# Seven late blocks of a SwiGLU down-projection by Strassen's seven products

## The chip, the core and the metric

The kernel runs on one core of a Trainium2 chip. Its engines work side by side and wait for each other by semaphores: TensorE (PE in the profile; PEld is its loading of weights), VectorE (DVE), ScalarE (ACT), GpSimd (POOL), and SyncE (SP), which here only starts DMAs. Matrix products go from SBUF into PSUM; VectorE and ScalarE read PSUM, GpSimd does not. The metric is device time in microseconds, lower is better. Before the change the median of three runs is 863.33 us (863.15 to 863.42).

## The reference

The input x is 8 batches of 3008 tokens with 256 channels. Each batch goes through a global filter along the tokens, then every token through a gated feed-forward layer:

```python
X = np.fft.rfft(x, axis=1)
Y = X * (filt_r + 1j * filt_i)[None]
y = np.fft.irfft(Y, n=x.shape[1], axis=1)          # (8, 3008, 256)

xn = y / sqrt(mean(y * y, -1) + 1e-6) * rms_g      # per token
g, val = xn @ w_gate, xn @ w_val                   # 256 -> 1536
out = (silu(g) * val) @ w_out                      # 1536 -> 256
```

The result is float32; the kernel's operands for matrix products are fp16 with fp32 sums.

## The kernel before

The filter is a two-stage Fourier transform (47 by 64) by matrix products with constant tables: `a_unit`, `b_unit` with `s_part` and `add_unit` (the multiplication by the filter), `bi_unit`, `n_unit`. It then squares and scales (`sq_unit`, `stat_unit`, `xt_unit`) and transposes by DMA (`tr_unit`) into `xn`, the feed-forward layer's input. This runs one batch ahead of the feed-forward layer and is woven into it.

The feed-forward layer is a list of 576 items (line 718): batch b (8), block m (6 per batch, 512 tokens each as four columns of 128; the last block of an even batch has three), inner tile jt (12 of 128 units, `JT`). One turn of the loop from line 837 handles a slot i:

- `gv(b, m, jt)` (line 533): two products of 512 columns each for gate and value (contraction 256 in two steps) into `pg` and `pv`, one PSUM bank each, two buffers each; Silu on ScalarE into `sg` (line 550); `hh = pv * sg` on VectorE (line 551), 128 inner units by 512 tokens, fp16, four buffers in turn.
- the units that the plan holds for this slot.
- `down` of the item two slots back (line 554): for each of the four token columns one product with `hh`'s 128x128 part as stationary operand and a row of `w_out` (256 columns) as the moving one, summed over jt in two PSUM banks `po0` and `po1`, which have one buffer each. The first one of a block is put off to the next slot, so that the banks' previous sums can be read out. After the twelfth, ScalarE copies one bank (line 568) and VectorE the other (line 569) into `o3`, and `o_store` puts the DMA to the output in SP's queue at a later slot.

The order of the work is fixed when the program is made. The plan (lines 718 to 830) gives each unit a slot, with costs per engine in microseconds in `load` and a limit per slot in `room`; a unit that does not fit moves to a later slot. Each engine takes its instructions in that order.

Memory: the pool `stg` has four buffers of 8 KB per partition. They hold the filter and gate and value weights during the load (`f_load`, `w_load`, both by DMAs from GpSimd's queue), later the fp32 tiles `y`, which use the first half of a buffer only (line 170). From line 610 the start is written out by hand; there `w_load(1)` stands behind `w_load(0)` (line 629).

The costliest names in the profile are line 546 (products of gate and value), 563 (down-projection), 551, 550, and on GpSimd 268 (`add_unit`), 330, 332 (`stat_unit`) and 340 (`xt_unit`).

Of the kernel before, what the change touches and what calls it, by code (L numbers as in the profile page):

```python
# [10 lines left out]
FP32 = mybir.dt.float32  # L11
FP16 = mybir.dt.float16
AXT = mybir.ActivationFunctionType
ALU = mybir.AluOpType
# [6 lines left out]
P = 128  # L21
D = 256
B = 8
DFF = 1536
JT = DFF // P
# [8 lines left out]
XC = 6  # L34
NXC = H // XC
KC = 8


def _make_tables():
# [62 lines left out]
def kernel(  # L102
# [11 lines left out]
    nc = tc.nc  # L114
# [6 lines left out]
    z_d = nc.dram_tensor("z_tmp", (B, K2, KR, D), FP16, kind="Internal").ap()  # L121

    glob = ctx.enter_context(tc.tile_pool(name="glob", bufs=1))
    stg = ctx.enter_context(tc.tile_pool(name="stg", bufs=4))
    xp = ctx.enter_context(tc.tile_pool(name="xp", bufs=4))
    t1p = ctx.enter_context(tc.tile_pool(name="t1p", bufs=3))
    t2p = ctx.enter_context(tc.tile_pool(name="t2p", bufs=3))
# [7 lines left out]
    hp = ctx.enter_context(tc.tile_pool(name="hp", bufs=4))  # L135
    op = ctx.enter_context(tc.tile_pool(name="op", bufs=2))
    psG = ctx.enter_context(tc.tile_pool(name="psG", bufs=2, space=bass.MemoryType.PSUM))
    psV = ctx.enter_context(tc.tile_pool(name="psV", bufs=2, space=bass.MemoryType.PSUM))
    psO = ctx.enter_context(tc.tile_pool(name="psO", bufs=1, space=bass.MemoryType.PSUM))
# [12 lines left out]
    wg = glob.tile([P, 2, DFF], FP16)  # L152
    wv = glob.tile([P, 2, DFF], FP16)
    wo = glob.tile([P, JT, D], FP16)
    gsb = glob.tile([P, 2], FP32)
    hhs = [glob.tile([P, 512], FP16, name="hh%d" % i) for i in range(4)]
    ss3 = [glob.tile([P, 4, 2, P], FP16, name="ss%d" % i) for i in range(3)]
# [6 lines left out]
    st = {b: {"x": {}, "t1": {}, "t2": {}, "s": {}, "yt": {}, "t4": {}, "y": {}, "sq": {},  # L164
              "u": {}, "xn": {}} for b in range(B)}

    def raw(src, row, ap):
        return bass.AP(tensor=src.tensor, offset=src.offset + row * D, ap=ap)

    def y_tile():  # L170
        t = stg.tile([P, 2, 4, 256], FP32, tag="stg", name="y")
        return t.rearrange("p a b c -> p (a b c)")[:, 0:1024].rearrange("p (a e) -> p a e", a=2)

    def x_load(b, c):
        t = xp.tile([P, XC, D], FP16, tag="xc", name="xc")
# [37 lines left out]
    def t2_tile(b, c):  # L213
        if b == 0 and c == 3:
            st[b]["t2"][c] = op.tile([KR, KC, D], FP16, tag="o3", name="t2o")
        else:
            st[b]["t2"][c] = t2p.tile([KR, KC, D], FP16, tag="t2", name="t2")

    def t2_load(b, c):
        t2_tile(b, c)  # L220
        nc.sync.dma_start(st[b]["t2"][c], z_d[b, c * KC:(c + 1) * KC, :, :].rearrange("k p d -> p k d"))

# [13 lines left out]
    def b_unit(b, i, bk=3, e=0):  # L236
        g, dh = divmod(i, 2)
        ps = bank(bk, "psb")[:, 0:4 * KR]
        for k in range(4):
            kk = 4 * g + k  # L240
            nc.tensor.matmul(ps[:, ts(k, KR)], st[b]["t2"][kk // KC][:, kk % KC, ds(dh * P, P)],  # L241
                             wb[0:KR, kk, :], start=True, stop=True)
# [128 lines left out]
        copy(eng, st[0]["t2"][c][:, 4 * r:4 * r + 4, :].rearrange("p k (e d) -> p k e d", e=2), ps)  # L371

    fst = {}
    FR4 = 4

    def f_load(i, f):
        if i not in fst:
            fst[i] = stg.tile([P, 2, FR4, D], FP32, tag="stg", name="fs")
        t = fst[i]
        row = FR4 * P * i if i < 2 else NF - 1 - FR4 * P  # L380
        for src in ((filt_i, filt_r)[f],):
            nc.gpsimd.dma_start(t[:, f].rearrange("p a d -> p (a d)"),
                                raw(src, row, [[FR4 * D, P], [1, FR4 * D]]))

    def f_unit(i, f, dh, e):
        t = fst[i]
        ps = bank(1 + "AV".index(e), "psf").rearrange("p (a q) -> p a q", a=FR4)
        for a in range(FR4):
            nc.tensor.transpose(ps[:, a, :], t[:, f, a, ds(dh * P, P)], idf)  # L389
        v = ps.rearrange("p a (q s) -> p s a q", s=16)  # L390
        fk = ff[:, dh, 0:K2].rearrange("p (t k) c -> p t k c", k=4)
        fu = ff[:, dh, 1:K2 + 1].rearrange("p (t k) c -> p t k c", k=4)[:, ::-1, ::-1, :]
        lo = SL * (1 + f) + 8 * i
        hi = lo + H
        if i < 2:
            copy(e, fk[:, :, :, lo:lo + 8], v[:, 0:8])
            copy(e, fu[:, :, :, hi:hi + 8], v[:, 8:16])
        else:
            copy(e, fk[:, :, :, lo:lo + 8], v[:, 8:16])
            copy(e, fu[:, :, :, hi:hi + 7], v[:, 0:8, :, 1:8])  # L400
# [6 lines left out]
    def f_neg(k0, n, dhs=(0, 1)):  # L407
        for dh in dhs:
            nc.gpsimd.tensor_scalar(out=ff[:, dh, k0:k0 + n, 0:SL], in0=ff[:, dh, k0:k0 + n, SL:2 * SL],
                                    scalar1=-1.0, scalar2=1.0, op0=ALU.mult, op1=ALU.mult)  # L410
# [102 lines left out]
    def scale_apply(m, bk):  # L513
# [12 lines left out]
                                    in1=y[:, h, :].rearrange("p (q e t) -> p q e t", q=2, e=2), op=ALU.mult)  # L526
        st[0]["xn"][m] = xn

    SPLIT = ((0, 0, 0), (B - 1, 5, JT - 1))
    hh_of = {}  # L530
    po_of = {}

    def gv(b, m, jt):
        n = nq(b, m)
        xn = st[b]["xn"][m]
        parts = ((0, 2), (2, 4)) if (b, m, jt) in SPLIT else ((0, n),)
        sg = hp.tile([P, 512], FP16, tag="sg", name="sg")
        hh = hhs[(6 * JT * b + JT * m + jt) % 4]
        made = []
        for q0, q1 in parts:  # L540
            w = (q1 - q0) * P
            pg = psG.tile([P, 512], FP32, tag="pg", name="pg")
            pv = psV.tile([P, 512], FP32, tag="pv", name="pv")
            for ps, wt in ((pg, wg), (pv, wv)):
                for dt_ in range(2):
                    nc.tensor.matmul(ps[:, 0:w], wt[:, dt_, ts(jt, P)], xn[:, q0:q1, dt_, :],  # L546
                                     start=(dt_ == 0), stop=(dt_ == 1))
            made.append((pg, pv, w, slice(q0 * P, q1 * P)))
        for pg, pv, w, c in made:
            nc.scalar.activation(out=sg[:, c], in_=pg[:, 0:w], func=AXT.Silu)  # L550
            nc.vector.tensor_tensor(out=hh[:, c], in0=pv[:, 0:w], in1=sg[:, c], op=ALU.mult)  # L551
        hh_of[(b, m, jt)] = hh

    def down(b, m, jt):
        hh = hh_of.pop((b, m, jt))
        if jt == 0:
            po_of[(b, m)] = [psO.tile([P, 2, D], FP32, tag="po%d" % i, name="po%d" % i)
                             for i in range(2)]
        po = po_of[(b, m)]

        n = nq(b, m)
        for s4 in range(n):
            nc.tensor.matmul(po[s4 // 2][:, s4 % 2, :], hh[:, ts(s4, P)], wo[:, jt, :],  # L563
                             start=(jt == 0 and s4 % 2 == 0),
                             stop=(jt == JT - 1 and (s4 % 2 == 1 or s4 == n - 1)))
        if jt == JT - 1:
            o3 = op.tile([P, 4, D], FP32, tag="o3", name="o3")
            nc.scalar.activation(out=o3[:, 0:2, :], in_=po[0], func=AXT.Copy)
            nc.vector.tensor_copy(out=o3[:, 2:n, :], in_=po[1][:, 0:n - 2, :])
            po_of[(b, m)] = o3  # L570
# [18 lines left out]

    def w_load(q):  # L590
        cols = ts(q, DFF // 3)
        t = stg.tile([P, 2, 2, DFF // 3], FP32, tag="stg", name="ws")
        for src, k in ((moe_w_gate, 0), (moe_w_val, 1)):
            nc.gpsimd.dma_start(t[:, k], src.rearrange("(dt p) j -> p dt j", p=P)[:, :, cols])
        wst[q] = t
# [14 lines left out]
    with tc.manual_schedule():  # L610
# [15 lines left out]
        nc.gpsimd.dma_start(wb[:, 0:4, :], wb_d[:, 0:4, :])  # L626
        nc.gpsimd.dma_start(wi, wi_d)
        w_load(0)
        w_load(1)
        nc.vector.memset(mhalf, -0.5)  # L630
        nc.vector.memset(ones, 1.0)
        for t in ss3[1:]:
# [29 lines left out]
        for g in range(7):  # L662
            tr0_unit(g, "V")
            if g < 6:
                f_unit(*todo[g + 2], "A")
        f_neg(4, 4, (0,))
        f_neg(8, 8, (0,))
        UN = K2 // 2
# [49 lines left out]
        items = [(b, m, jt) for b in range(B) for m in range(6) for jt in range(JT)]  # L718
        plan, late = {}, {}
        front = (sq_unit, s_part, add_unit)  # L720
        load = {r: [0.0] * (len(items) + 99) for r in "MBAV"}
        room = {"A": 0.8, "V": 0.7}
        for i in range(JT + 1, len(items), JT):
            load["A"][i] = 0.6
            load["V"][i] = 0.68

        def at(slot, fn, *a):
            todo = (late if fn == q_unit else plan).setdefault(slot, [])
            if fn in front:
                todo.insert(0, (fn, a))  # L730
            else:
                todo.append((fn, a))
# [77 lines left out]
        for b in range(1, B):  # L810
            t = (b - 1) * 72
# [20 lines left out]
        for i, now in plan.items():  # L832
            if any(fn == a_unit and a[3] == 0 for fn, a in plan.get(i + 1, ())) and bi_unit in [fn for fn, _ in now]:
                now.sort(key=lambda u: u[0] == sq_unit)

        stores = {}
        for i in range(len(items) + 4):
            if i < len(items):
                gv(*items[i])
            for fn, a in plan.pop(i, ()):  # L840
                fn(*a)
            if 2 <= i < len(items) + 2:
                b, m, jt = items[i - 2]
                if jt == 1 and i > JT:
                    down(b, m, 0)
                if jt or i < JT:
                    down(b, m, jt)
                if items[i - 2][2] == JT - 1:
                    stores[i + 1] = items[i - 2][:2]
            for fn, a in late.pop(i, ()):  # L850
                fn(*a)
            if i in stores:
                o_store(*stores[i])
# [31 lines left out]
```

## Time and profile before

| what | value |
|---|---|
| median of three runs | 863.33 us |
| span of the profiled execution (first to last instruction) | 861.4 us |
| PE, PEld busy | 852.4, 532.2 us |
| DVE, ACT, POOL busy | 557.2, 612.4, 297.8 us |
| mean granted TensorE clock | 0.999 |
| DMA | 107.98 MB, mean 125 GB/s |

The page lists no time of the profiled execution beside its span, so the median stands for it: 1.9 us lie around the span. Busy times are sums over the span; engines overlap. In a line of the timeline the columns are start, length in microseconds, engine, line of the kernel, instruction, what it writes and reads with shapes and types, and how many; in square brackets stands the idle time of the engine before it and what ended it. A product's length in these lines includes its way through the array; products that follow one another start sooner than that.

### The profile page before, as it was taken

To read this page: it belongs to the slowest core of one execution; us is meant where nothing else is said; L and a number is where in the kernel's file an instruction comes from. 1 tells how busy PE (TensorE), PEld (TensorE's weight loads), DVE (VectorE), ACT (ScalarE), POOL (GpSimd) and SP (SyncE) were. 2 spreads that over 40 slices of the span, in tenths; PEclk is the share of its full clock that TensorE was granted. 3 is DMA by queue.
4 is the path that set the end of the run, shared out by engine and by line. 5 is a ranking of instruction groups with operands and counts; after the bars stand their busy time and mean duration, and the time that the engine had idled before them with its cause. 6 is when DMAs were issued, how large, how long until landed. Compare 5 with 4: busy or idle time off the path is not lost.

```text
span 861.4 us, 17024 instructions
## 1 busy us (share of the span) xinstructions
PE 852.4 (99%) x6142; PEld 532.2 (62%) x6142; DVE 557.2 (65%) x926; ACT 612.4 (71%) x1339; POOL 297.8 (35%) x346
## 2 busy tenths in 40 slices
PE   8999999999999999999999999999999999999997
PEld 6755666566666666666666666666666666665664
DVE  5857655776666666666666676767666665555554
ACT  4986777787588756887577856888567765777443
POOL 5725742453144322534034430444123430132000
PEclk9999999999999999999999999999999999999999
DMA  9995778765975476656755548433564331521101
GB/s 283 270 204 124 150 164 168 139 130 121 197 137 129 121 150 111 151 107 147 139 127 113 132 98 180 108 87 101 131 127 93 97 70 42 124 54 49 62 25 50
DMA packets 198237, 107.98 MB, mean 125 GB/s; under 512 B 158566, under 2 KB 182520, under 8 KB 198152
## 3 DMA queue, kind: packets, MB, share of 16 engines
q1 hardware_dynamic: 189464, 85.52, 44.1%
q0 software_dynamic: 8544, 21.24, 12.7%
q8 instruction: 48, 0.79, 0.4%
q14 instruction: 37, 0.30, 0.1%
q10 hardware_dynamic: 144, 0.13, 0.0%
HBM read 45.78 MB, written 35.65 MB: 95 GB/s over the span
## 4 chain that ended last, share of the span: by engine, by line
PE 96%; DMA 1%; ACT 1%; DVE 1%; issue 0%; POOL 0%; POOLq 0%
PE po L563 28%; PE pg L546 28%; PE pv L546 28%; PE psb L241 3%; PE psi L285 3%; PE psn L314 2%; PE psa L206 2%; DMA fs<-in_filt_i_dram 1%; PE psy L418 1%; PE psf L389 1%; PE pst L367 0%; ACT sg L550 0%; POOL xc L186 0%; DVE s L231 0%; DVE hh L551 0%
## 5 line engine op out<-in xcount | busy, mean ns | idle before, releaser
L551 DVE TENSOR_TENSOR hh<-pv,sg 128x512 f16<-128x512 f32 (+2 forms) x578 | 391.5, 678 | 286.4 <-ACT sg L550 221.9
L550 ACT ACTIVATE sg<-pg 128x512 f16<-128x512 f32 (+2 forms) x578 | 337.4, 584 | 217.6 <-PE pg L546 213.4
L546 PE MATMUL pg<-xn,wg 128*128 128x512 f16 (+2 forms) x1156 | 338.1, 374 | 0.1
L546 PE MATMUL pv<-xn,wv 128*128 128x512 f16 (+2 forms) x1156 | 338.1, 374 | 0.0
L563 PE MATMUL po<-wo,hh 128*128 128x256 f16 x2256 | 332.7, 273 | 0.0
L563 PEld LDWEIGHTS <-hh 128*128 128x128 f16 x2256 | 213.4, 98 | 105.5 <-issue 0.6
L268 POOL TENSOR_TENSOR ss<-s,s 128x384 f16<-128x384 f16 x112 | 101.9, 911 | 273.2 <-DVE s L234 245.2
L546 PEld LDWEIGHTS <-wv 128*128 128x128 f16 x1156 | 112.9, 98 | 130.7
L546 PEld LDWEIGHTS <-wg 128*128 128x128 f16 x1156 | 111.4, 98 | 17.0 <-issue 0.3
L340 POOL TENSOR_TENSOR xt<-y,rho 128x1024 f16<-128x1024 f32 (+1 forms) x46 | 85.4, 1856 | 2.8
L322 ACT ACTIVATE junk<-y 128x256 f16<-128x256 f32 x180 | 74.3, 413 | 2.8
L231 DVE TENSOR_TENSOR s<-psb,ff 128x384 f16<-128x384 f32 x124 | 67.6, 547 | 0.7 <-ACT ff L195 0.6
L234 DVE TENSOR_TENSOR s<-psb,ff 128x384 f16<-128x384 f32 x124 | 67.6, 546 | 0.0
L195 ACT ACTIVATE uu<-psi 128x384 f16<-128x384 f32 (+1 forms) x127 | 61.6, 486 | 1.5 <-DMA out_dram<-o 0.5
L195 ACT ACTIVATE y<-psn 128x512 f32<-128x512 f32 (+1 forms) x95 | 55.7, 588 | 4.2
L285 PEld LDWEIGHTS <-yt 96*128 96x128 f16 x512 | 35.4, 97 | 26.7 <-issue 1.0
L332 POOL TENSOR_TENSOR rho<-u,mhalf 128x4 f32<-128x4 f32 (+1 forms) x46 | 46.5, 1010 | 3.8
L330 POOL TENSOR_SCALAR u<-ss 128x4 f32<-128x4 f32 (+1 forms) x46 | 8.9, 193 | 104.8 <-ACT junk L322 103.8
L195 ACT ACTIVATE t<-psa 128x512 f16<-128x512 f32 x70 | 41.4, 594 | 3.1 <-PE psa L206 1.7
L285 PE MATMUL psi<-wi,yt 96*128 96x96 f16 x512 | 42.9, 205 | 0.1
L241 PE MATMUL psb<-wb,t 96*128 96x96 f16 x480 | 40.1, 206 | 0.3 <-DVE s L234 0.2
L241 PEld LDWEIGHTS <-t 96*128 96x128 f16 x480 | 28.7, 97 | 12.8 <-DVE s L234 3.3
(101 smaller groups left out, 366.2 us busy)
## 6 DMA issues: line engine op xcount, KB each, us to landing
out_dram<-o SPq DMA_DIRECT2D x40, 512.0 KB, 3.6
xc<-in_x_dram POOLq DMA_DIRECT2D x31, 384.0 KB, 5.6
z_tmp<-t SPq DMA_DIRECT2D x28, 384.0 KB, 2.7
t<-z_tmp SPq DMA_DIRECT2D x28, 384.0 KB, 6.0
out_dram<-o SPq DMA_DIRECT2D x7, 384.0 KB, 2.7
fs<-in_filt_i_dram POOLq DMA_DIRECT2D x3, 512.0 KB, 10.8
fs<-in_filt_r_dram POOLq DMA_DIRECT2D x3, 512.0 KB, 11.2
ws<-in_moe_w_gate_dram POOLq DMA_DIRECT2D x3, 512.0 KB, 9.8
```

What stands on the lines that cost most here:

```text
L195: nc.scalar.activation(out=out, in_=in_, func=AXT.Copy, **({} if scale is None else {"scale": scale}))
L231: eng.tensor_tensor(out=o, in0=ps, in1=f1, op=ALU.mult)
L234: eng.tensor_tensor(out=o, in0=ps[:, :, ::-1, :], in1=f2, op=ALU.mult)
L241: nc.tensor.matmul(ps[:, ts(k, KR)], st[b]["t2"][kk // KC][:, kk % KC, ds(dh * P, P)], wb[0:KR, kk, :], start=True, stop=True)
L268: nc.gpsimd.tensor_tensor(out=ss3[g % 3][:, :, dh, 0:KR], in0=s[0], in1=s[1], op=ALU.add)
L285: nc.tensor.matmul(ps[:, k, :], yt[0:KR, k, dh, :], wi[0:KR, 4 * g + k, :], start=True, stop=True)
L322: nc.scalar.activation(out=junk, in_=y[:, i, ts(u, D)], func=AXT.Square, accum_out=ss[:, 2 * i + u:2 * i + u + 1])
L340: nc.gpsimd.tensor_tensor(out=xt[:, 0:n, :], in0=y.rearrange("p a (u d) -> p (a u) d", u=2)[:, 0:n, :], in1=rho[:, 0:n].unsqueeze(2).to_br ...
L546: nc.tensor.matmul(ps[:, 0:w], wt[:, dt_, ts(jt, P)], xn[:, q0:q1, dt_, :], start=(dt_ == 0), stop=(dt_ == 1))
L550: nc.scalar.activation(out=sg[:, c], in_=pg[:, 0:w], func=AXT.Silu)
L551: nc.vector.tensor_tensor(out=hh[:, c], in0=pv[:, 0:w], in1=sg[:, c], op=ALU.mult)
L563: nc.tensor.matmul(po[s4 // 2][:, s4 % 2, :], hh[:, ts(s4, P)], wo[:, jt, :], start=(jt == 0 and s4 % 2 == 0), stop=(jt == JT - 1 and (s4 ...
```

## The change

In seven blocks, (6,3), (6,4) and (7,0) to (7,4), the items of a block are walked in two halves of two token columns (256 tokens), six pairs of inner tiles each. An item is now two inner tiles by two token columns, and its down-projection, a 2x2 by 2x2 block product (token columns by inner tiles, inner tiles by output halves of 128 channels), is made by Strassen's seven products in place of eight. The number of items, 12 per block, stays.

- `gv_seven` makes the gate and value of an item with eight products of 256 columns, then Silu and hh as before, and three further VectorE instructions, all on fp16 in SBUF: the sums and differences of hh's parts (two of 256 elements per partition, one of 128).
- `w_seven` makes the five sums of parts of `w_out` once, on GpSimd, at slots 372 to 420.
- `down_seven` makes seven products of 128 columns. After a half's last one, ScalarE copies 128 and 512 columns out of PSUM, VectorE makes one sum and GpSimd three to get the output's four parts. The first down-projection of each half is put off by a slot, so the output banks change hands twice a block. The store is issued at slot i+3 where it was i+1.
- The plan's `load` gets 0.56 more on VectorE for each such item and 0.7 on ScalarE once per block.
- The four `stg` buffers become four fixed tiles `big`, used in the same turn; the sums lie in their second halves. `w_load(1)` is issued after the first batch's filter units.

```diff
+    big = [glob.tile([P, 2 * FR4 * D], FP32, name="big%d" % i) for i in range(4)]
+    spare = [t[:, FR4 * D:] for t in big]
+    half = [t.bitcast(FP16) for t in spare]
...
+    SEVEN = {(B - 2, m) for m in (3, 4)} | {(B - 1, m) for m in range(5)}
+
+    def w_seven(n):
+        v = wo.rearrange("p (i j) (e d) -> p i j e d", j=2, e=2)
+        f, a, b = ((ALU.add, (0, 0), (1, 1)), (ALU.subtract, (0, 1), (1, 1)), (ALU.subtract, (1, 0), (0, 0)),
+                   (ALU.add, (0, 0), (0, 1)), (ALU.add, (1, 0), (1, 1)))[n]
+        nc.gpsimd.tensor_tensor(out=ws7[n], in0=v[:, :, a[0], a[1], :], in1=v[:, :, b[0], b[1], :], op=f)
+
+    def gv_seven(b, m, jt):
+        half, jp = divmod(jt, JP)
...
+        for ps, wt in ((pg, wg), (pv, wv)):
+            for j in range(2):
+                for dt_ in range(2):
+                    nc.tensor.matmul(ps[:, ts(j, 2 * P)], wt[:, dt_, ts(2 * jp + j, P)],
+                                     xn[:, 2 * half:2 * half + 2, dt_, :], start=(dt_ == 0), stop=(dt_ == 1))
+        nc.scalar.activation(out=sg, in_=pg, func=AXT.Silu)
+        nc.vector.tensor_tensor(out=hh, in0=pv, in1=sg, op=ALU.mult)
+        a = hh.rearrange("p (s t) -> p s t", s=4)
...
+        nc.vector.tensor_tensor(out=hs[:, 0:2], in0=a[:, 0:2], in1=a[:, 3:4].to_broadcast([P, 2, P]), op=ALU.add)
+        nc.vector.tensor_tensor(out=hs[:, 2:4], in0=a[:, 1:3], in1=a[:, 0:4:3], op=ALU.subtract)
+        nc.vector.tensor_tensor(out=h5, in0=a[:, 0], in1=a[:, 2], op=ALU.add)
+        hh_of[(b, m, jt)] = (a, hs, h5)
+
+    def down_seven(b, m, jt):
...
+        mm(pb[:, 0], a[:, 0], ws7[1][:, jp], **first)
+        mm(pb[:, 1], a[:, 3], ws7[2][:, jp], **mid)
+        mm(pa[:, 0], hs[:, 0], ws7[0][:, jp], **first)
+        mm(pb[:, 3], hs[:, 1], w[:, 0, 0], **mid)
+        mm(pa[:, 2], hs[:, 2], ws7[3][:, jp], **mid)
+        mm(pa[:, 1], hs[:, 3], ws7[4][:, jp], **last)
+        mm(pb[:, 2], h5, w[:, 1, 1], **last)
+        if jp == JP - 1:
+            o = o3_of[(b, m)][:, 2 * half:2 * half + 2, :].rearrange("p q (e d) -> p (q e) d", e=2)
+            t = osum
+            nc.scalar.activation(out=t[:, 4], in_=pa[:, 0], func=AXT.Copy)
+            nc.scalar.activation(out=t[:, 0:4], in_=pb, func=AXT.Copy)
+            nc.vector.tensor_tensor(out=o[:, 0:4:3], in0=pa[:, 1:3], in1=t[:, 4:5].to_broadcast([P, 2, P]), op=ALU.add)
+            nc.gpsimd.tensor_tensor(out=o[:, 1:3], in0=t[:, 0:2], in1=t[:, 2:4], op=ALU.add)
+            nc.gpsimd.tensor_tensor(out=t[:, 2:4], in0=t[:, 1::-1], in1=t[:, 2:4], op=ALU.subtract)
+            nc.gpsimd.tensor_tensor(out=o[:, 0:4:3], in0=o[:, 0:4:3], in1=t[:, 2:4], op=ALU.add)
...
-        w_load(1)
...
+        w_load(1)
         f_neg(4, 4, (0,))
...
+        for b, m in SEVEN:
+            for jt in range(JT):
+                load["V"][6 * JT * b + JT * m + jt] += 0.56
+            load["A"][6 * JT * b + JT * m + JP + 1] += 0.7
...
+        for n in range(5):
+            at(372 + 12 * n, w_seven, n)
...
+                seven = (b, m) in SEVEN
+                fn, n = (down_seven, JP) if seven else (down, JT)
+                if jt % n == 1 and i > JT:
+                    fn(b, m, jt - 1)
+                if jt % n or i < JT:
+                    fn(b, m, jt)
+                if jt == JT - 1:
+                    stores[i + (3 if seven else 1)] = (b, m)
```

More of the change, by code (lines that the diff above doesn't have):

```diff
@@ L36 @@
 KC = 8
+FR4 = 4
 def _make_tables():
@@ L123 @@
     glob = ctx.enter_context(tc.tile_pool(name="glob", bufs=1))
-    stg = ctx.enter_context(tc.tile_pool(name="stg", bufs=4))
     xp = ctx.enter_context(tc.tile_pool(name="xp", bufs=4))
@@ L154 @@
     wo = glob.tile([P, JT, D], FP16)
+    big = [glob.tile([P, 2 * FR4 * D], FP32, name="big%d" % i) for i in range(4)]
+    spare = [t[:, FR4 * D:] for t in big]
+    half = [t.bitcast(FP16) for t in spare]
+    ws7 = [half[n // 2][:, ts(n % 2, JT // 2 * P)].rearrange("p (i d) -> p i d", d=P) for n in range(5)]
+    hs4 = [(half[0][:, 1536:], half[1][:, 1536:], half[3][:, 0:512], half[3][:, 512:1024])[i]
+           .rearrange("p (s t) -> p s t", s=4) for i in range(4)]
+    hs1 = [half[3][:, 1024 + i * P:1024 + (i + 1) * P] for i in range(4)]
+    osum = spare[2][:, 384:1024].rearrange("p (s t) -> p s t", s=5)
     gsb = glob.tile([P, 2], FP32)
@@ L168, in raw, with big_tile @@
         return bass.AP(tensor=src.tensor, offset=src.offset + row * D, ap=ap)
+    turn = [0]
+    def big_tile():
+        turn[0] += 1
+        return big[(turn[0] - 1) % 4]
     def y_tile():
-        t = stg.tile([P, 2, 4, 256], FP32, tag="stg", name="y")
-        return t.rearrange("p a b c -> p (a b c)")[:, 0:1024].rearrange("p (a e) -> p a e", a=2)
+        return big_tile()[:, 0:FR4 * D].rearrange("p (a e) -> p a e", a=2)
     def x_load(b, c):
@@ L373 @@
     fst = {}
-    FR4 = 4
     def f_load(i, f):
         if i not in fst:
-            fst[i] = stg.tile([P, 2, FR4, D], FP32, tag="stg", name="fs")
+            fst[i] = big_tile().rearrange("p (f a d) -> p f a d", f=2, a=FR4)
         t = fst[i]
@@ L527, in scale_apply @@
         st[0]["xn"][m] = xn
+    JP = JT // 2
+    SEVEN = {(B - 2, m) for m in (3, 4)} | {(B - 1, m) for m in range(5)}
[4 more added lines that the diff above has]
+        nc.gpsimd.tensor_tensor(out=ws7[n], in0=v[:, :, a[0], a[1], :], in1=v[:, :, b[0], b[1], :], op=f)
@@ new lines, in gv_seven @@
+    def gv_seven(b, m, jt):
+        half, jp = divmod(jt, JP)
+        xn = st[b]["xn"][m]
+        sg = hp.tile([P, 512], FP16, tag="sg", name="sg")
+        hh = hhs[(6 * JT * b + JT * m + jt) % 4]
+        pg = psG.tile([P, 512], FP32, tag="pg", name="pg")
+        pv = psV.tile([P, 512], FP32, tag="pv", name="pv")
+        for ps, wt in ((pg, wg), (pv, wv)):
[6 more added lines that the diff above has]
+        a = hh.rearrange("p (s t) -> p s t", s=4)
+        n = (6 * JT * b + JT * m + jt) % 4
+        hs, h5 = hs4[n], hs1[n]
+        nc.vector.tensor_tensor(out=hs[:, 0:2], in0=a[:, 0:2], in1=a[:, 3:4].to_broadcast([P, 2, P]), op=ALU.add)
+        nc.vector.tensor_tensor(out=hs[:, 2:4], in0=a[:, 1:3], in1=a[:, 0:4:3], op=ALU.subtract)
+        nc.vector.tensor_tensor(out=h5, in0=a[:, 0], in1=a[:, 2], op=ALU.add)
+        hh_of[(b, m, jt)] = (a, hs, h5)
@@ new lines, in down_seven @@
+    def down_seven(b, m, jt):
+        a, hs, h5 = hh_of.pop((b, m, jt))
+        half, jp = divmod(jt, JP)
+        if jt == 0:
+            o3_of[(b, m)] = op.tile([P, 4, D], FP32, tag="o3", name="o3")
+        if jp == 0:
+            po_of[(b, m)] = [psO.tile([P, 2, D], FP32, tag="po%d" % i, name="po%d" % i)
+                             .rearrange("p a (e d) -> p (a e) d", e=2) for i in range(2)]
+        pa, pb = po_of[(b, m)]
+        first, mid, last = dict(start=(jp == 0), stop=False), dict(start=False, stop=False), \
+            dict(start=False, stop=(jp == JP - 1))
+        w = wo[:, 2 * jp:2 * jp + 2, :].rearrange("p j (e d) -> p j e d", e=2)
+        mm = nc.tensor.matmul
+        mm(pb[:, 0], a[:, 0], ws7[1][:, jp], **first)
[14 more added lines that the diff above has]
+            nc.gpsimd.tensor_tensor(out=o[:, 0:4:3], in0=o[:, 0:4:3], in1=t[:, 2:4], op=ALU.add)
+            po_of[(b, m)] = o3_of[(b, m)]
@@ L529 @@
     SPLIT = ((0, 0, 0), (B - 1, 5, JT - 1))
+    o3_of = {}
     hh_of = {}
@@ L591, in w_load @@
         cols = ts(q, DFF // 3)
-        t = stg.tile([P, 2, 2, DFF // 3], FP32, tag="stg", name="ws")
+        t = big_tile().rearrange("p (k e j) -> p k e j", k=2, e=2)
         for src, k in ((moe_w_gate, 0), (moe_w_val, 1)):
@@ L838 @@
             if i < len(items):
-                gv(*items[i])
+                (gv_seven if items[i][:2] in SEVEN else gv)(*items[i])
             for fn, a in plan.pop(i, ()):
@@ L843 @@
                 b, m, jt = items[i - 2]
[L844 to L849, printed above, removed]
+                seven = (b, m) in SEVEN
[6 more added lines that the diff above has]
+                    stores[i + (3 if seven else 1)] = (b, m)
             for fn, a in late.pop(i, ()):
```

## The prediction

> **What bounds the kernel now.** I read the page first (busy shares, chain of waits), then the busy times of each engine in the stretches that the changed blocks occupy, then single instructions in the timeline for prices.
>
> From the page of the kernel before: span, busy times, chain by engine.
> ```profile
> span 861.4 us, 17024 instructions
> PE 852.4 (99%) x6142; PEld 532.2 (62%) x6142; DVE 557.2 (65%) x926; ACT 612.4 (71%) x1339; POOL 297.8 (35%) x346
> PE 96%; DMA 1%; ACT 1%; DVE 1%; issue 0%; POOL 0%; POOLq 0%
> ```
> TensorE is the bound: it makes 96% of the chain, so a nanosecond off its work counts as long as nobody makes it wait. The reader should also note the other shares: VectorE is idle only a third of the time.
>
> Busy time in five of the seven changed blocks (stretch, its length, then PE, PEld, DVE, ACT, POOL with instruction counts):
> ```profile
> 716.47:732.59 16.12, 16.12 (x109) 9.89 (x108) 9.35 (x15) 9.17 (x16) 1.20 (x2) 1.00 0.20 56
> 732.59:748.73 16.14, 16.14 (x101) 9.71 (x100) 8.92 (x14) 11.13 (x24) 3.10 (x3) 1.00 0.58 125
> 761.43:777.46 16.03, 16.03 (x98) 9.48 (x97) 8.58 (x13) 11.70 (x28) 6.19 (x6) 1.00 0.19 42
> 777.46:793.71 16.25, 16.25 (x100) 9.67 (x99) 8.80 (x13) 11.86 (x28) 3.09 (x3) 1.00 0.26 66
> 809.31:824.91 15.60, 15.60 (x97) 9.38 (x96) 8.90 (x14) 7.76 (x13) 0.00 (x0) 1.00 0.09 34
> ```
> I put the borders at the first Silu of blocks (6,3), (6,4), (7,0), (7,1) and (7,3). (7,2) and (7,4), from 793.71 and 824.91, also last 15.60. TensorE is busy all through at full clock. A bare block is 15.60 us, 1.300 per item; the first four carry 0.43 to 0.65 of other units. VectorE has about 6.7 to 7.5 us free per block: that is the room that the new work has to fit in.
>
> Prices, from the timeline (start, length, engine, line):
> ```profile
> 7.86 1.06 PE L357 MATMUL psa<-tab,xc 128*128 128x128 f16 x16
> 830.34 0.60 PE L563 MATMUL po<-wo,hh 128*128 128x256 f16 x4
> 825.54 0.69 DVE L551 TENSOR_TENSOR hh<-pv,sg 128x512 f16<-128x512 f32 x1 [0.61 <-ACT sg L550]
> 55.31 0.16 DVE L509 CAST hl<-rho 128x4 f16<-128x4 f32 x1
> 55.50 0.16 DVE L510 TENSOR_TENSOR hl<-rho,hl 128x4 f16<-128x4 f32 x1
> 19.99 1.28 DVE L197 COPY t2o<-pst 96x1024 f16<-96x1024 f16 x2 [0.20 <-PE pst L367]
> 26.25 0.55 DVE L234 TENSOR_TENSOR s<-psb,ff 128x384 f16<-128x384 f32 x1
> 26.71 0.55 DVE L231 TENSOR_TENSOR s<-psb,ff 128x384 f16<-128x384 f32 x1
> ```
> Sixteen 128-column products, each with its own weight load, start (1.06 - 0.219)/15 = 0.056 apart. The four 256-column products start (0.60 - 0.273)/3 = 0.109 apart. The 1.300 of an item then leaves (1.300 - 4 x 0.109)/4 = 0.216 for a 512-column product. On VectorE, 384 elements with fp32 operands start 0.46 apart, while 1024 fp16 elements start 1.28 - 0.68 = 0.60 apart: some 0.065 fixed, plus 1.04 ns per element, or half that where all is fp16. Line 510 reads what line 509 wrote and starts 0.03 after its end.
>
> **The change, part by part.** TensorE. An item (two inner tiles by 256 tokens) had four products of 512 columns and four of 256: 1.300. It gets eight of 256 and seven of 128: 8 x 0.109 + 7 x 0.056 = 1.264. That saves 0.036, and over 84 items 3.0 us. Doubling the weight loads of gate and value costs nothing by the 256-column row (one load per product there already); nor do seven loads in the down-projection, by the 128-column row. The Trainium skill speaks against this: "TensorE: Matmul & The Clock Gate", section "Back-to-back issue gap", gives about 81 ns per product for a stream of loads and 128-column products. By that rule the seven would take 0.567, an item 1.439, and the kernel would lose 12 us; this trace, with 56 ns in a stream of just that kind, does not agree, and the measurement decides.
>
> VectorE, per item. Added are two adds of 256 fp16 elements and one of 128, all operands in SBUF. No row has a two-operand fp16 form. One element per step bounds them above: 2 x 0.331 + 0.198 = 0.86. The fixed part alone bounds them below: 3 x 0.065 = 0.20. I take two per step, 2 x 0.198 + 0.132 = 0.53, since the fp16 copy, nearest in type, runs so. The first add reads hh, so it waits for its end: 0.69 + 0.03 instead of 0.61 until VectorE is free. An item is then 0.72 + 0.53 = 1.25. Per block the 512-element copy of the output (0.61) goes and two 256-element adds (0.33 each) come. A block is 12 x 1.25 + 0.66 = 15.66 on VectorE. On TensorE it becomes 0.43 shorter: 15.69, 15.71, 15.60, 15.82 and three times 15.17. So TensorE paces the first four, or nearly; in the three bare blocks VectorE is the longer by 0.49 each. With 0.06 from (7,0) that is 1.5, less what VectorE may lag before anybody waits. That is least at a handover of the output banks, which now comes twice a block: bank po0 is wanted again two gate-value groups and two products later, 2 x 0.872 + 0.11 = 1.86, and in the meantime come the drain (0.17), ScalarE's 128-column copy (some 0.27, from 0.594 for 512 and 0.486 for 384) and, as VectorE gets there about 1.24 after the last product, the 0.33 add: 0.3 spare. 1.5 - 0.3 = 1.2 us come back.
>
> ScalarE. Per half two copies (0.17 and 0.49 to the next start) replace one of 0.49 per block: 0.8 more per block on 7.8 to 11.9 of 16, room enough. But a pair of squares (0.41 + 0.19 each) holds a Silu up to 1 us now, which hh hid in VectorE's idle time. With that idle time gone, part of it comes through: seven pairs in the second run of changed blocks, 0 to 0.3 each, 0 to 2 us; I take 0.9, as hh is then late already and half of it overlaps.
>
> GpSimd. Three fp32 adds of 256 elements per half: xt takes 1.892 for 1024 and 1.465 for 768, so about 0.18 + 256 x 1.67 ns = 0.61 each. They use 4 of 15 us per block beside at most 6.2, feed only the store, and cost nothing by themselves. The five weight sums (768 fp16 elements; 0.911 for 384 makes 1.6 each) fall in slots 372 to 420, ahead of queued ss adds. The yt transposes behind these then land 1.6 later; the one that landed at 596.35 is first read at 600.87, so 4.5 hides 1.6. Without that cover it would be 1.6 each, 8 us.
>
> Queues and places. The store goes two slots later on SP; behind it wait only xn transposes with ten slots to spare. The second weight load keeps its place in GpSimd's queue, after the first load and ahead of line 409's work, and waits for the same readers: nothing. The staging ring has four buffers in the same order; the sums lie in the half that y does not use. Working the planner's formula with the added loads moves no unit. The Silu and hh work itself is unchanged in size.
>
> Sum: -3.0 + 1.2 + 0.9 = -0.9. The span of 861.4 becomes 860.5. The median of the runs shown is 863.33, 1.9 above this span; I leave that as it is: 862.4.
>
> **The rivals.** First, faster: VectorE keeps up everywhere. It decides at (15.17 - 0.66)/12 = 1.21 per item, that is adds 0.04 cheaper than mine together. The fixed part of 0.065 is from instructions with a PSUM operand, and these have none. Then only TensorE's 3.0 counts: 860.4.
>
> Second, slower: GpSimd holds VectorE up. Every VectorE instruction of weight so far has at most one operand in SBUF; each new add has two. If such an add cannot start while a GpSimd instruction runs, then only hh (0.72) covers it. A norm's rho (1.01) and xt (1.89) leave 0.29 + 1.17 = 1.46 or more; five of these sets lie in or at the end of changed blocks: 7.3. The first two output adds (1.22) run beside the 0.33 add and hh (1.05) and leave 0.2, the third, if it gets in between the new adds, 0.6: 0.2 to 0.8 in each of 14 halves, 2.8 to 11. Together 10 to 18, and 873 when the lower end holds. For it: VectorE has no idle time left to take it in. Against it: hh keeps 0.69 beside any GpSimd work, but it has only one SBUF operand, so the trace says nothing for two. The Trainium skill states it: "SBUF — State Buffer", section "SBUF: two separate sides": "The shared pair is an exclusive lock, not a bandwidth split", with a VectorE instruction of two SBUF inputs among those that need it. No row here shows that.
>
> Third, slower: the adds go one element per step. An item is 1.58, a block 19.6, some 4 us more than TensorE's in each of seven: 889. Against it stands the fp16 copy.
>
> Fourth, the output handover misses its 0.3: half a microsecond in 14 halves, 7 us, 869. Against it: line 568 and 569's copies of twice the size held no product up before.
>
> **How the numbers follow.** My forecast (VectorE just at TensorE's pace, 861 to 865) has 0.40; faster 0.22; GpSimd 0.29; one per step 0.05; handover or dearer products 0.04. What a measurement can tell from no change is 0.2%, 1.7 us: 861.6 to 865.1. Of the forecast's 0.40, 0.11 lies below that, 0.23 inside and 0.06 above. So faster 0.33, same 0.23, slower 0.44. The range reaches from the first rival's 860.4 to 876, past the second's 873; above lie the upper half of the second and the third, some 0.15, below 0.04.
>
> **What would show it.** TensorE: products of 256 and 128 columns 0.109 and 0.056 apart, an unheld item of 1.264. VectorE: the 256-element adds near 0.28 long (0.20 apart) at two per step, 0.41 at one; about 15.7 busy-to-busy per block with no idle time in (7,2) to (7,4), and hh there no longer waiting for Silu. If TensorE shows no idle time after 716, the first rival holds; if adds start late or stretch whenever xt or the output adds run, the second does. Idle time of TensorE before the first product of a half whose releaser is the 0.33 add or a copy speaks for the fourth. I am wrong on the mechanism if TensorE's idle time in changed blocks has any releaser other than VectorE's hh or adds.

## The result and the profile after

The changed kernel takes 878.54 us (878.34 to 878.95), the kernel before 863.24: 15.3 us slower, a ratio of 1.0177 (1.0163 to 1.0192). The forecast of 862.4 and its range up to 876.0 are both missed; of the prediction's cases the second rival, GpSimd holding VectorE up, is the one that came near.

The page of the changed kernel: span, busy times, chain by engine.

```profile
span 876.8 us, 18550 instructions
PE 853.5 (97%) x6730; PEld 565.2 (64%) x6730; DVE 620.8 (71%) x1185; ACT 617.8 (70%) x1360; POOL 338.6 (39%) x393
PE 87%; DVE 8%; issue 2%; ACT 1%; DMA 1%; POOL 0%; DVEq 0%; POOLq 0%
```

TensorE's share of the chain fell from 96% to 87%, and VectorE now holds 8%. The stretches of blocks (6,3), (6,4), (7,0), (7,1) and (7,3), from first Silu to first Silu as before:

```profile
716.43:732.86 16.43, 16.01 (x188) 14.57 (x187) 15.90 (x48) 9.84 (x19) 3.50 (x5) 1.00 0.19 54
732.86:750.37 17.51, 16.26 (x183) 14.19 (x182) 17.09 (x49) 11.73 (x27) 7.33 (x9) 1.00 0.62 117
763.94:781.95 18.01, 16.02 (x177) 14.23 (x176) 16.94 (x44) 12.26 (x31) 8.16 (x9) 1.00 0.15 39
781.95:802.06 20.11, 17.21 (x185) 14.43 (x184) 19.69 (x54) 12.75 (x31) 8.40 (x10) 1.00 0.21 53
820.83:838.54 17.71, 15.49 (x182) 14.16 (x181) 17.29 (x52) 8.48 (x17) 4.64 (x6) 1.00 0.08 31
```

Every changed block is longer than it was (16.12, 16.14, 16.03, 16.25, 15.60). In the first four the loss grows with GpSimd's work: 3.5 us of POOL go with 0.3 us lost, 8.4 with 3.9. The bare block loses 2.1 us at only 4.6 us of POOL; there TensorE has no other units' work. The clock is full throughout. VectorE's records fill nearly the whole time, 17.29 of 17.71 in the bare block. Block (6,5), which has no adds, starts behind a late VectorE and takes 13.57 in place of 12.70. Up to item 468 the two traces agree to 0.04 us, so all of the loss arises from there on, and the weight sums, the moved load and the fixed tiles cost nothing that shows.

The new adds by line, with minimum, median and maximum length in ns:

```profile
L567 DVE TENSOR_TENSOR big<-hh x84: 291/293/2021, 717.8 to 856.9; 128x256 f16<-128x256 f16 x84
L568 DVE TENSOR_TENSOR big<-hh x84: 277/284/1975, 718.0 to 857.1; 128x256 f16<-128x256 f16 x84
L569 DVE TENSOR_TENSOR big<-hh x84: 210/218/1916, 718.2 to 857.3; 128x128 f16<-128x128 f16 x84
```

The medians are those of two elements per step (0.29 for 256 elements, where 0.28 was forecast at two and 0.41 at one). The maxima are not a matter of size. The timeline shows what stands beside the longest ones. VectorE first, then GpSimd:

```profile
806.44 0.68 DVE L563 TENSOR_TENSOR hh<-pv,sg 128x512 f16<-128x512 f32 x1
807.15 0.57 DVE L567 TENSOR_TENSOR big<-hh 128x256 f16<-128x256 f16 x1
807.65 1.98 DVE L568 TENSOR_TENSOR big<-hh 128x256 f16<-128x256 f16 x1
809.55 0.21 DVE L569 TENSOR_TENSOR big<-hh 128x128 f16<-128x128 f16 x1
```

```profile
805.98 0.79 POOL L599 TENSOR_TENSOR big<-big 128x256 f32<-128x256 f32 x1
806.85 0.73 POOL L600 TENSOR_TENSOR o<-o,big 128x256 f32<-128x256 f32 x1
807.53 1.94 POOL L353 TENSOR_TENSOR xt<-big,rho 128x1024 f16<-128x1024 f32 x1
```

The first add lasts until 807.72, some 0.15 after the output sum of line 600 has ended; the second until 809.63, some 0.15 after xt. hh at 806.44 runs beside the same GpSimd work at its usual 0.68. Over all 252 adds, 35 are longer than the median of their line by more than 0.03 us, 17.0 us in sum: 7.1 us by five of them beside xt, 9.8 by 29 beside the output sums, and 0.1 by one beside a GpSimd copy (line 305).

How TensorE comes to wait:

```profile
842.23 0.22 PE L586 MATMUL po<-big,hh 128*128 128x128 f16 x1
843.55 0.22 PE L587 MATMUL po<-big 128*128 128x128 f16 x1 [1.10 <-DVE o L597]
843.61 0.22 PE L588 MATMUL po<-wo,big 128*128 128x128 f16 x1
```

The third product of a new half writes the bank that VectorE's output add (line 597) has yet to read; held adds in front of it make it late: the adds of lines 567 and 569 there last 0.59 and 0.74 in place of 0.29 and 0.22. This wait alone sums to 9.3 us in 12 halves.

### The profile page after: what moved, and what is told of

Same layout as the page of the kernel before. It is cut to its first block, busy times and chain, and to the rows that moved or that the text cites. A ratio compares the mean times of both kernels' runs of the same rounds, so it can differ in the third digit from the quotient of the medians.

```text
span 876.8 us, 18550 instructions
## 1 busy us (share of the span) xinstructions
PE 853.5 (97%) x6730; PEld 565.2 (64%) x6730; DVE 620.8 (71%) x1185; ACT 617.8 (70%) x1360; POOL 338.6 (39%) x393
## 4 chain that ended last, share of the span: by engine, by line
PE 87%; DVE 8%; issue 2%; ACT 1%; DMA 1%; POOL 0%; DVEq 0%; POOLq 0%
PE po L638 24%; PE pg L621 23%; PE pv L621 23%; DVE hh L563 3%; PE psb L254 3%; PE psi L298 2%; PE psa L219 2%; PE psn L327 2%; DVE big L568 2%; PE pg L560 2%; PE pv L560 2%; DVE big L569 1%; DMA big<-in_filt_i_dram 1%; PE psy L430 1%; PE psf L401 1%
## 5 line engine op out<-in xcount | busy, mean ns | idle before, releaser
L626 DVE TENSOR_TENSOR hh<-pv,sg 128x512 f16<-128x512 f32 (+2 forms) x494 | 333.6, 676 | 234.6 <-ACT sg L625 177.5
L621 PE MATMUL pg<-xn,wg 128*128 128x512 f16 (+2 forms) x988 | 287.9, 373 | 0.1
L621 PE MATMUL pv<-xn,wv 128*128 128x512 f16 (+2 forms) x988 | 287.8, 373 | 0.0
L353 POOL TENSOR_TENSOR xt<-big,rho 128x1024 f16<-128x1024 f32 (+1 forms) x46 | 85.5, 1859 | 2.8
L562 ACT ACTIVATE sg<-pg 128x512 f16<-128x512 f32 x84 | 50.1, 597 | 49.7 <-DVE big L569 24.5
L335 ACT ACTIVATE junk<-big 128x256 f16<-128x256 f32 x180 | 74.4, 413 | 2.8
L208 ACT ACTIVATE big<-psn 128x512 f32<-128x512 f32 (+1 forms) x95 | 55.7, 588 | 5.0 <-PE psn L327 0.8
L563 DVE TENSOR_TENSOR hh<-pv,sg 128x512 f16<-128x512 f32 x84 | 57.3, 682 | 1.1 <-ACT sg L562 0.9
L560 PE MATMUL pv<-xn,wv 128*128 128x256 f16 x336 | 50.4, 272 | 0.7 <-DVE hh L563 0.7
L560 PE MATMUL pg<-xn,wg 128*128 128x256 f16 x336 | 50.4, 273 | 0.0
```

The lines of the kernel that those rows point to most:

```text
L208: nc.scalar.activation(out=out, in_=in_, func=AXT.Copy, **({} if scale is None else {"scale": scale}))
L335: nc.scalar.activation(out=junk, in_=y[:, i, ts(u, D)], func=AXT.Square, accum_out=ss[:, 2 * i + u:2 * i + u + 1])
L353: nc.gpsimd.tensor_tensor(out=xt[:, 0:n, :], in0=y.rearrange("p a (u d) -> p (a u) d", u=2)[:, 0:n, :], in1=rho[:, 0:n].unsqueeze(2).to_br ...
L560: nc.tensor.matmul(ps[:, ts(j, 2 * P)], wt[:, dt_, ts(2 * jp + j, P)], xn[:, 2 * half:2 * half + 2, dt_, :], start=(dt_ == 0), stop=(dt_ = ...
L563: nc.vector.tensor_tensor(out=hh, in0=pv, in1=sg, op=ALU.mult)
```

## The experiments

Theory A: an add with both operands in SBUF is held while a GpSimd instruction runs. Theory B: no hold; VectorE simply has more work than fits, and lateness shows wherever it waits. Theory C: the handover of the output banks by ScalarE's copies is late. All times below are medians; the kernel before ran beside them at 863.2.

**Without the output sums.**

```diff
-            nc.scalar.activation(out=t[:, 0:4], in_=pb, func=AXT.Copy)
+            nc.scalar.activation(out=o, in_=pb, func=AXT.Copy)
...
-            nc.gpsimd.tensor_tensor(out=o[:, 1:3], ...)
-            nc.gpsimd.tensor_tensor(out=t[:, 2:4], ...)
-            nc.gpsimd.tensor_tensor(out=o[:, 0:4:3], ...)
```

> Left out: GpSimd's three output sums per half; ScalarE copies the second bank straight into the output tile instead, same size, so the output lacks those terms. VectorE's and TensorE's work is unchanged. Theory A (an add with two SBUF operands is held while a GpSimd instruction runs): in the changed kernel the adds that ran beside output sums were longer than undisturbed ones by 9.9 us in all, those beside xt by 7.1; the first part goes: 878.5 - 9.9 = 868.6, and the adds of the two bare blocks are all 0.29 or less. Theory B (VectorE has simply too much work, and the long adds are only where its lateness shows): VectorE's work is as before, so 877 to 879. Theory C (the handover of the output banks is late because of ScalarE's copies): the copies stay, 877 to 879.

870.63 us, a ratio of 1.0085 (1.0070 to 1.0100): 7.9 us of the 15.3 gone, although VectorE has the same work. The two bare blocks without an xt, (7,3) and (7,4), fell from 17.7 to 15.82 us. B and C expected no gain. The gain is 2 us under A's 9.9; the adds beside xt are still held, 8.5 us in sum, 1.4 more than before, which can account for most of the rest.

**xt on ScalarE.**

```diff
+        nc.scalar.activation(out=xt[:, q, :], in_=y[:, q // 2, ts(q % 2, D)], func=AXT.Copy, scale=rho[:, q:q + 1])
...
+                if b == B - 1 and fn == xt_unit:
+                    for q in range(4):
+                        at(s + d + q, xt_part, b, m, q)
```

> The normalised tile xt of the last batch's six blocks is made by ScalarE in four instructions of 256 elements, one per slot, in place of one GpSimd instruction of 1.89 us. Theory A: the 7.1 us that adds ran longer beside xt go, less up to 1.5 for Silu held by the new ScalarE work: 871.4 to 873. Theory B and C: no gain, ScalarE's 1.2 us more per norm can only cost: 878 to 880.

874.53 us, 1.0131 (1.0116 to 1.0146): 4.0 us faster than the changed kernel, where A said 5.5 to 7.1. The time that adds are held fell from 17.0 to 10.8 us, which is 6.2 less. Where the other 2.2 us went this run does not show in full. Part of it went to ScalarE's new work: TensorE waits 0.26 us for a Silu in block (6,5), which has no adds and still takes 13.41 us against 12.70 before the change. The alternate halves below show how.

**Both.**

> Both edits together, the output again without GpSimd's sums. Theory A: all 17.0 us of longer adds go, 878.5 - 17.0 = 861.5, up to 863 with Silu held at times: about the time of the kernel before, as the forecast's sum without the hold has it (862.4). VectorE then has 15.2 us of items and 0.7 us of output adds per block. Theory B and C: 877 to 880.

864.43 us, 1.0015 (1.0006 to 1.0025). No add is longer than its undisturbed length any more:

```profile
L578 DVE TENSOR_TENSOR big<-hh x84: 291/292/293, 717.8 to 842.5; 128x256 f16<-128x256 f16 x84
```

14.1 of the 15.3 us are gone with the same number of adds, of ScalarE's copies out of PSUM and of products. A's 861.5 to 863 is missed by 1.4; block (6,5) with ScalarE's parts takes 13.77, 1.1 more than before. B and C fall: VectorE's work and the copies are all still there.

**One operand in PSUM.** This leaves GpSimd's work beside the adds alone and puts one operand of each add into PSUM. The adds treat half as many elements, at one per step, so VectorE's time stays equal.

```diff
+            px.append(bank(3, "psx"))
+            nc.tensor.matmul(px[0], wg[:, 0, 0:P], wg[:, 0, 0:512], start=True, stop=True)
+        p2 = px[0][:, 0:P].rearrange("p (s t) -> p s t", s=2)
-        nc.vector.tensor_tensor(out=hs[:, 0:2], in0=a[:, 0:2], in1=a[:, 3:4].to_broadcast([P, 2, P]), op=ALU.add)
+        nc.vector.tensor_tensor(out=hs[:, 0:2, 0:64], in0=p2, in1=a[:, 0:2, 0:64], op=ALU.add)
...
```

> GpSimd's work stays in full. The three adds per item take their first operand from a PSUM bank that is free by then (constant contents, so the output is wrong) and treat half as many elements, so that at one element per step they take the same VectorE time as before (0.20 + 0.20 + 0.13 to the next start), with one operand in SBUF instead of two. Theory A: no add is held, all have one length whatever GpSimd does; 861.5 to 863. Theory B and C: the same VectorE time per item, so 877 to 879.

862.31 us, 0.9988 (0.9978 to 0.9998). GpSimd's sums and xt are all there, and no add is held. Two of its lines, and a stretch in which an add (828.91) runs beside an output sum (828.83):

```profile
L577 DVE TENSOR_TENSOR big<-psx,hh x84: 290/291/293, 718.1 to 840.5; 128x128 f16<-128x128 f32 x84
L579 DVE TENSOR_TENSOR big<-psx,hh x84: 211/214/216, 718.5 to 840.9; 128x64 f16<-128x64 f32 x84
```

```profile
828.91 0.29 DVE L577 TENSOR_TENSOR big<-psx,hh 128x128 f16<-128x128 f32 x1
829.12 0.28 DVE L578 TENSOR_TENSOR big<-psx,hh 128x128 f16<-128x128 f32 x1
```

```profile
828.83 0.73 POOL L610 TENSOR_TENSOR o<-o,big 128x256 f32<-128x256 f32 x1
```

Same count, same length, same GpSimd work, 16 us apart: where the operands lie decides. With the second SBUF operand the edit also takes away the two elements per step, and no run separates these fully. Two per step alone brought no hold in the one case at hand: in the changed kernel an fp16 copy from PSUM at two per step (line 210, at 20.55) lasts its usual 0.68 beside a GpSimd instruction that reads SBUF (line 421, 20.55 to 21.06). An instruction at two per step with a single SBUF operand was not run. B is refuted here once more: with this VectorE load the kernel is as fast as the kernel before.

What is left of VectorE's load shows at the handover of the output banks. Here, with no add held, VectorE's output add (line 607) ends at 828.28, and the third product of the half starts 0.32 after the second, where products follow at 0.056:

```profile
827.87 0.41 DVE L607 TENSOR_TENSOR o<-po,big 128x256 f32<-128x256 f32 x1
828.02 0.22 PE L596 MATMUL po<-big,hh 128*128 128x128 f16 x1
828.34 0.22 PE L597 MATMUL po<-big 128*128 128x128 f16 x1
```

**Without the adds.**

```diff
-        nc.vector.tensor_tensor(out=hs[:, 0:2], ...)
-        nc.vector.tensor_tensor(out=hs[:, 2:4], ...)
-        nc.vector.tensor_tensor(out=h5, ...)
+        hs, h5 = a, a[:, 1]
```

> Left out: VectorE's three adds per item; the seven products read parts of hh directly, so the output is wrong. TensorE's products, the weight sums, the output adds on VectorE and GpSimd and the copies stay. It measures TensorE's term by itself. By the forecast's prices the products save 3.0 us and nothing else is on the path: 863.2 - 3.0 = 860.2. If the handover of the banks or the doubled weight loads cost something by themselves (theory C), it is above 861.5.

859.9 us, 0.9962 (0.9948 to 0.9975): 3.3 us saved, where 3.0 was expected. Bare blocks take 15.17 us, as forecast. Neither the doubled weight loads nor the bank handover costs anything that shows while VectorE is on time, so C falls too. GpSimd's instructions beside a VectorE that makes no two-SBUF-operand adds cost nothing that shows either.

**GpSimd writing only.**

```diff
+            for k in range(3):
+                nc.gpsimd.memset(t, 0.0)
```

> As the run without GpSimd's output sums (870.6), with three GpSimd memsets of 640 fp32 elements per half in their place: GpSimd then writes SBUF and reads nothing. If the hold comes from GpSimd's reading, the adds beside memsets keep their 0.29, 0.28 and 0.22 and the time stays at 870 to 871.5. If any GpSimd work in SBUF holds them, adds beside memsets are longer by up to a memset's length and the time goes up to 873 to 880.

869.96 us, 1.0077 (1.0063 to 1.0091). That is 0.7 under the run without the sums, and the adds beside xt, the only ones held, are held 7.8 us in place of 8.5. Three memsets beside the adds, then the adds:

```profile
835.95 2.01 POOL L599 MEMSET big<- 128x640 f32 x3 [5.91 <-DVE o L597]
```

```profile
836.52 0.29 DVE L567 TENSOR_TENSOR big<-hh 128x256 f16<-128x256 f16 x1
836.73 0.28 DVE L568 TENSOR_TENSOR big<-hh 128x256 f16<-128x256 f16 x1
836.93 0.22 DVE L569 TENSOR_TENSOR big<-hh 128x128 f16<-128x128 f16 x1
```

45 adds run beside memsets alone, the longest of each line 293, 286 and 220 ns. So a GpSimd instruction that only writes SBUF holds no add. All those that did hold one, xt, the three sums and the copy of line 305, read a block of SBUF.

**Alternate halves,** xt on GpSimd and xt on ScalarE.

```diff
+        if half:
+            hh_of[(b, m, jt)] = a
+            return
...
+        for j in range(2):
+            for q in range(2):
+                nc.tensor.matmul(po[:, q], a[:, 2 * j + q], wo[:, 2 * jp + j, :], ...)
```

> In each of the seven blocks only the first half uses the seven products; the second half uses four products of 256 columns per item, and no adds, into one bank that ScalarE copies out. GpSimd's output sums of a first half then run while VectorE makes no adds. TensorE saves 6 x 0.036 and pays 6 x 0.012 for shorter products per block, 0.15, 1.0 us in all. Theory A: only the adds beside xt are held, up to 1.7 each where they fall in a first half, and VectorE has idle time in the second halves to take part of it: 862.2 to 865. Theory B (too much work): VectorE's work falls by 42 x 0.53, so it keeps up as well, but there GpSimd does not matter and it is 862.2 with xt on GpSimd or not.

> As the run with alternate halves, and the last batch's xt on ScalarE in four parts, so that no GpSimd instruction of length is left beside adds. Theory A: no add is longer than 0.30; 862.2, or up to 863.2 where ScalarE's parts hold a Silu. Theory B: the same as with xt on GpSimd, or up to 1 more.

865.37 us, 1.0027 (1.0017 to 1.0036), and 864.03, 1.0009 (1.0000 to 1.0018). With xt on GpSimd only three adds are held, 1.91 us long each, all beside xt; the output sums disturb nothing now. The bare blocks take 15.45, under the 15.60 of before. The three held adds stand in the blocks that got longer: (7,0) 17.63, (7,1) 16.77, (7,2) 16.25. With xt on ScalarE no add is held, but the time misses 862.2 to 863.2 by 0.8: (6,4) takes 16.67 and (6,5) 13.39, where they take 15.98 and 12.71 with xt on GpSimd. ScalarE's part of xt comes between the squares and a Silu, and TensorE's next gate product waits for that Silu:

```profile
750.45 0.49 ACT L364 ACTIVATE xt<-big,rho 128x256 f16<-128x256 f32 x1
750.85 0.47 ACT L655 ACTIVATE sg<-pg 128x384 f16<-128x384 f32 x1
751.37 0.48 PE L651 MATMUL pg<-xn,wg 128*128 128x384 f16 x2 [0.47 <-ACT sg L655]
```

With three shorter stops of the kind, before the products at 751.96, 760.42 and 761.01, this makes up the 1.4 us of the two blocks. So xt costs time in both places: on GpSimd it holds adds, on ScalarE it delays a Silu. The last version moves the adds instead.

**Chosen halves.**

```diff
+    WHICH = {(B - 2, 3): 0, (B - 2, 4): 0, (B - 1, 1): 0, (B - 1, 2): 1, (B - 1, 3): 1, (B - 1, 4): 1}
+    SEVEN = set(WHICH)
...
+                at(s + d + 2 * (fn == xt_unit and (b, m) == (B - 1, 4)), fn, b, m)
```

> One half with the seven products in six blocks, the other plain, and the half chosen so that no xt runs beside adds: the first half in (6,3), (6,4) and (7,1), the second in (7,2) to (7,4), none in (7,0); (7,4)'s xt is issued two slots later, and xt stays on GpSimd. Theory A: no add is longer than 0.30, a bare block is 15.45 instead of 15.60, and the time is 863.2 - 6 x 0.15 = 862.3, at or just below the kernel before. Theory B: nothing but VectorE's amount of work counts, so it is as good as the alternate halves with xt on GpSimd in the way, that is 865.

862.36 us, 0.9989 (0.9980 to 0.9998), 0.9 us under the kernel before and 16.2 under the changed one. No add is held:

```profile
L573 DVE TENSOR_TENSOR big<-hh x36: 216/217/220, 718.6 to 840.8; 128x128 f16<-128x128 f16 x36
```

B had said 865. It keeps the whole computation and uses the seven products in 36 items rather than 84, so it has 0.9 of the 3.3 us that they can give. A gain of 0.1% is small; its interval lies just clear of none.

## Why the prediction was wrong

**TensorE's term was right.** 0.109 and 0.056 per product came out as such (in the timeline the products from 843.55 on start 0.05 to 0.06 apart), and the run without adds measures 3.3 us for the forecast 3.0. The 81 ns that the Trainium skill gives ("TensorE: Matmul & The Clock Gate", section "Back-to-back issue gap") for a 128-column product with its load have no support here: they would have made bare blocks longer, and without the adds these went to 15.17.

**VectorE's own price was right.** The choice of two elements per step, taken from the fp16 copy, holds: 256 elements last 0.29 and start 0.20 apart, an undisturbed item is 1.26 against 1.25 forecast. Without the hold a bare block takes 15.66 with the PSUM operand and 15.82 without sums, against 15.66. What comes back was also put in the right place, the handover of the output banks: the third products of the halves in the three bare blocks come 1.3 us late in sum with the PSUM operand and 2.1 us with the real adds in the run of both edits, where 1.2 was forecast. That the kernel with the PSUM operand takes 862.31, so near the forecast's 862.4, is partly luck: the products gave 3.3 for 3.0, no wait shows the 0.9 of a delayed Silu, and this run has one more product than the change (line 575), which with the wait before it costs some 0.5 us.

**The step that failed** is the one on GpSimd: that the output sums "feed only the store, and cost nothing by themselves", and with it that an add costs VectorE 0.53 per item whatever runs beside it. The adds were held 17.0 us, 0.2 per item on average. The sums also last 0.73 to 0.80 each, on average by line, where 0.61 was forecast. On a VectorE with no idle time most of the 17.0 reached TensorE: 862.4 + 17.0 = 879.4 is within 1 us of 878.5. The second rival had the mechanism and priced it at 10 to 18 us; in it, rho was put at 0.29 or more per set and held nothing, xt at 1.17 or more and held 1.41 on average (7.1 in five), and the output sums at 2.8 to 11 and held 9.8. The mistake is in the weighing. It got 0.29 because no row before the change could show it. But the prediction itself gave reasons to rank it higher: no VectorE instruction of weight had two SBUF operands, so the undisturbed hh beside GpSimd was no evidence against, and the forecast had just used up the idle time that could have hidden it. And its lower end, 873, was used as its time and set the top of the range.

**The other terms put at nothing** cost nothing that shows: the weight sums, the weight load, the later store, the doubled weight loads, since the run without adds has them all and saves the 3.3. The 0.9 for a Silu delayed by squares has no wait to show for it; a delayed Silu does reach TensorE in the runs with ScalarE's new parts, where block (6,5) grew by up to 1.1 us.

**The third and fourth rival** are out. Adds go two elements per step. The sign that was named for the fourth did appear, 9.3 us of waits behind the output add, but without holds these waits shrink to the 1.3 and 2.1 us above, so the handover is where the holds reach TensorE and not their cause.

The rule of the Trainium skill, "SBUF — State Buffer", section "SBUF: two separate sides", agrees in its main point: a VectorE instruction with two SBUF inputs and a GpSimd one that reads SBUF do not run together (1.98 us for an add beside an xt of 1.94), and the hold is gone with one input in PSUM or with GpSimd memsets, which only write. That a GpSimd instruction keeps VectorE out for its whole length does not hold for rho: eight adds beside rho alone, 1.0 us long, kept 0.28 to 0.29 and 0.22.

## What to carry to other kernels

Before moving arithmetic to VectorE, look where its operands lie: an instruction with both inputs in SBUF can wait for a GpSimd instruction that reads a block of SBUF, and the profile shows this only as a longer instruction, with no wait and no releaser. Price such an instruction by GpSimd's busy time beside it when VectorE has no idle time left; place the two in different stretches, as the chosen halves do, or give it an operand in PSUM, which here doubled its time per element. When a rival's mechanism has no row for or against it, its chance should follow from what is new in the change, not from the missing row.

## What the runs showed of the hardware

Held adds end 0.08 to 0.15 us after the GpSimd instruction that held them, and the records count the waiting as their length. The hold seems to work both ways a little: the output sum of line 599 lasts 0.724 to 0.855 beside adds, and 0.73 in the kernels without adds or with a PSUM operand. GpSimd's memsets and its rho (four elements per partition, 1.02 us) hold nothing. An add of 128 elements with an fp32 operand in PSUM lasts 0.291, one of 256 fp16 elements from SBUF 0.293: half the elements in the same time.
